# A decode block on one core: TensorE's and VectorE's programs inside a loop of two turns whose first turn jumps over the body, and six filler products for ten

## The chip, the cores and the metric

The kernel runs on one NeuronCore of a Trainium2 chip. The core has five engines that run programs of their own and meet at semaphores: TensorE (PE in the profile, with its weight loads as PEld), VectorE (DVE), ScalarE (ACT), GpSimd (POOL) and SyncE (SP, which here only issues DMAs). [...] 

The metric is the device time of one execution, in microseconds. Before the change the median of 3 runs is 1276.88 us (1276.62 to 1277.0).

## What is computed

One decode step of a transformer block for 4 sequences (B = 4, one new token each, D = 512): layer norm, attention over a cache of 8192 positions with 32 heads of width 128, a residual, a second layer norm, a gated unit of width 1792, and a second residual.

```python
def _A_ref(x, k_cache, v_cache, wq, wo):          # x is normed, (4, 1, 512)
    q = (x @ wq).reshape(B, Sq, 32, 128).transpose(0, 2, 1, 3)
    scores = jnp.einsum("bhqd,bhkd->bhqk", q, k_cache) * (128 ** -0.5)
    o = jnp.einsum("bhqk,bhkd->bhqd", softmax(scores), v_cache)
    return o.transpose(0, 2, 1, 3).reshape(B, Sq, 4096) @ wo
def _B_ref(x, w_gate, w_up, w_down):
    return (sigmoid(x @ w_gate) * (x @ w_up)) @ w_down
h = x + _A_ref(layernorm(x), k_cache, v_cache, wq, wo)
return h + _B_ref(layernorm(h), w_gate, w_up, w_down)
```

All tensors are bfloat16. The two caches hold 4 x 32 x 8192 x 128 elements each; with the weights, each execution has to read 550.77 MB.

## The kernel before, in words

**Data.** The 128 pairs of sequence and head are worked in 32 units of four heads. A unit's K is one DMA, and so is its V. Three slots (`KV`) take them: K alternates between slots 0 and 1, V goes to slot 2, and the last V to slot 0. SP issues everything in one hand-written order: `wq` first (line 532), then K and V units in turn (line 541), each behind a wait until its slot is free, then 40 empty instructions, and at the end `wo` (line 546), `w_gate` (548), `w_up` (552) and `w_down` in three pieces of eight, four and two of its fourteen column tiles (557).

**A unit.** VectorE transposes K in 16 chunks (line 335), TensorE multiplies each with the query (344), VectorE and ScalarE make the softmax (362 to 369), VectorE transposes the weights (375). TensorE multiplies the weights of the unit before with its V (405); ScalarE scales the result (410) and TensorE adds it into one bank (415).

**The programs.** Each engine's instructions are collected in a list (`_Prog.list`), and at the end `play` writes each list into that engine's own program, once. TensorE's and VectorE's programs hold loops over the units: TensorE's body is one unit, 31 turns, with a small loop for the 16 chunks in it; VectorE's is two units, 15 turns. The first unit, the last one (for VectorE) and all that follows the attention stand behind or ahead of these loops as straight code. An engine's program therefore has a start (layer norm, query projection), a loop in which nearly all the time passes, and an end.

**The end.** After the last K unit TensorE runs 24 filler products (`filler(2, 12)`: a product of constants into an unused bank, two in each turn of a small loop, line 388), multiplies the last V (405), lays the attention's output out (415, 454, 461, 466), runs ten filler products (`filler(2, 5)`, called at line 467), multiplies with `wo` (475), adds the residual (479, 480), runs ten more (`filler(2, 5)`, line 481), and goes on with the second layer norm (273 to 287), the gate and up products (492), the sigmoid (503), the product of the two with its transposes in two halves (509, 512) and the product with `w_down` (521), whose fourteen tiles wait for the three pieces of `w_down`. VectorE and ScalarE copy the result (529, 530), ScalarE issues the output DMA (559), and SP waits for it.

Of the kernel before, what the change touches and what calls it, by code (L numbers as in the profile page):

```python
# [18 lines left out]
class _Prog:  # L19
# [52 lines left out]
    def emit(self, eng, fn, waits=(), incs=1, ch=None):  # L72
        todo = self._waits(eng, waits)
        key = ch or eng
        tok = self.token(key, incs) if incs else None
        self._put(eng, todo, key, fn, incs, 1)
        return tok
# [41 lines left out]
def bass_sequential_preLN__mha_block_cached__glu_gated_glu__decode_kernel(  # L119
# [34 lines left out]
    prog = _Prog({"p2d": "dve", "d2d": "dve", "a2d": "dve", "d2p": "pe", "a2p": "pe",  # L154
                  "d2a": "act", "p2a": "act",
                  "k0": "dve", "k1": "dve", "v2": "pe"})
    emit = prog.emit

    with ExitStack() as es:
# [222 lines left out]
        def filler(n, turns=1):  # L382
            if turns > 1:
                prog.open("pe")
            for _ in range(turns):
                if turns > 1:
                    prog.begin("pe")
                emit("pe", lambda e: [e.matmul(bank[XS], Lq[:, 0:128], Lq[:, 0:512], start=True, stop=True) for _ in range(n)][-1],  # L388
                     [t_ps0, t_lq[NU - 1]], incs=0)
                if turns > 1:  # L390
                    prog.end("pe")
            if turns > 1:
                prog.close("pe")
# [70 lines left out]
            return ins  # L464
        t_rt = emit("pe", f, [t_oa])
        t_ot = emit("dve", lambda e: e.tensor_copy(OT, bank[QB[0]][:, 0:B * WOJ]), [t_rt])
        filler(2, 5)

        emit("act", lambda e: e.activation(dummy[:, 0:1], mask[:, 0:1], ACT.Sqrt), [t_mask])

# [89 lines left out]
        emit("sp", lambda e: e.nop(), [t_out], incs=0)  # L560

        for name, e in (("pool", nc.gpsimd), ("act", nc.scalar), ("dve", nc.vector), ("pe", nc.tensor), ("sp", nc.sync)):
            prog.play(nc, name, e)


# [26 lines left out]
```

## Time and profile before

| what | value |
|---|---|
| median of 3 runs | 1276.88 us |
| the profiled execution's own time | 1276.83 us |
| its span, first to last instruction | 1275.6 us |
| mean granted TensorE clock | 0.815 |
| PE, PEld, DVE, ACT, POOL busy | 61%, 26%, 60%, 5%, 0% |
| bytes moved, mean rate | 550.83 MB, 432 GB/s |

The profile is of one execution. Its span starts with the first instruction of the kernel and ends with the last; the execution's own time is 1.23 us longer. Times in the timeline and in the chain of waits are microseconds from the start of the span: first the start, then the duration. In brackets stands how long the engine had been idle and what ended it. A view of windows cuts the span into stretches and gives for each the busy time of the engines, the granted TensorE clock (1.00 is full speed), the mean busy share of the sixteen DMA engines and the rate.

### The profile page before, as it was taken

To read this page: it belongs to the slowest core of one execution; us is meant where nothing else is said; L and a number is where in the kernel's file an instruction comes from. 1 tells how busy PE (TensorE), PEld (TensorE's weight loads), DVE (VectorE), ACT (ScalarE), POOL (GpSimd) and SP (SyncE) were. 2 spreads that over 40 slices of the span, in tenths; PEclk is the share of its full clock that TensorE was granted. 3 is DMA by queue.
4 is the path that set the end of the run, shared out by engine and by line. 5 is a ranking of instruction groups with operands and counts; after the bars stand their busy time and mean duration, and the time that the engine had idled before them with its cause. 6 is when DMAs were issued, how large, how long until landed. Compare 5 with 4: busy or idle time off the path is not lost.

```text
span 1275.6 us, 14073 instructions
## 1 busy us (share of the span) xinstructions
PE 779.7 (61%) x4588; PEld 328.5 (26%) x4636; DVE 762.3 (60%) x917; ACT 59.0 (5%) x114; POOL 5.7 (0%) x22
## 2 busy tenths in 40 slices
PE   1676755557755557655567655567555577555577
PEld 0232222223222223222222222222222232222233
DVE  1876665556665557665567655566655566655571
ACT  2000000000000000000000000000000000000001
POOL 1000000000000000000000000000000000000000
PEclk8888877788877788877788777788777888777888
DMA  9999999999999999999999999999999999999998
GB/s 423 432 426 430 427 450 434 430 430 427 454 430 430 430 427 454 432 427 430 430 452 432 427 430 434 450 430 427 430 440 444 430 427 430 442 442 430 430 427 371
DMA packets 10244, 550.83 MB, mean 432 GB/s; under 512 B 1144, under 2 KB 1152, under 8 KB 1408
## 3 DMA queue, kind: packets, MB, share of 16 engines
q1 hardware_dynamic: 10224, 550.77, 99.7%
q8 instruction: 2, 0.03, 0.0%
q10 hardware_dynamic: 16, 0.01, 0.0%
q14 instruction: 2, 0.02, 0.0%
HBM read 550.77 MB, written 0.00 MB: 432 GB/s over the span
## 4 chain that ended last, share of the span: by engine, by line
DMA 60%; PE 20%; DVE 12%; issue 2%; ACT 1%; SPq 0%; DVEq 0%
DMA KV<-in_A_k_cache_dram 58%; PE PS L344 14%; DVE kT L335 12%; PE PS L405 5%; DMA KV<-in_B_w_down_dram 3%; ACT kT L410 1%; PE PS L415 0%; SPq L541 0%; DVE PTz L375 0%; PE PS L521 0%; DVE KV L529 0%; SPq L557 0%; DVEq L112 0%
## 5 line engine op out<-in xcount | busy, mean ns | idle before, releaser
L344 PE MATMUL PS<-kT,Lq 128*128 128x512 bf16 x2048 | 588.7, 420 | 343.5 <-DVE kT L335 326.4
L335 DVE STREAM_TRANSPOSE kT<-KV 128x1024 f32<-128x1024 f32 x512 | 614.4, 1232 | 300.3 <-DMA KV<-in_A_k_cache_dram 237.5
L344 PEld LDWEIGHTS PS<-kT,Lq 128*128 x2048 | 210.3, 103 | 694.6 <-issue 621.7
L375 DVE STREAM_TRANSPOSE PTz<-E_sb 32x512 bf16<-32x512 bf16 x128 | 89.9, 703 | 129.1 <-PE PS L415 125.5
L405 PE MATMUL PS<-KV,PTz 128*16 128x512 bf16 x2048 | 117.0, 381 | 0.0
L379 PE MATMUL PS<-part,headw 128*128 128x2 f32 x64 | 18.8, 363 | 100.4 <-DVE PTz L375 100.4
L369 ACT ACTIVATE E_sb<-PS,negm 128x512 bf16<-128x512 f32 x32 | 22.0, 687 | 1139.4 <-DVE negm L367 1139.4
L405 PEld LDWEIGHTS PS<-KV,PTz 128*16 128x16 bf16 x2048 | 58.9, 111 | 56.3 <-issue 13.6
L415 PE MATMUL PS<-lane,kT 128*128 128x4 f32 x256 | 33.6, 255 | 31.0 <-ACT kT L410 31.0
L362 DVE TENSOR_REDUCE part<-PS 128x1 f32<-128x512 f32 x32 | 22.1, 691 | 38.7 <-PE PS L344 38.7
L415 PEld LDWEIGHTS PS<-lane,kT 128*128 128x128 f32 x256 | 31.0, 191 | 46.2 <-issue 44.8
L379 PEld LDWEIGHTS PS<-part,headw 128*128 128x128 f32 x64 | 16.0, 310 | 103.7 <-DVE PTz L375 103.7
L410 ACT ACTIVATE kT<-PS,rsb 128x512 f32<-128x512 f32 x32 | 22.0, 687 | 61.5 <-PE PS L405 61.5
L388 PE MATMUL PS<-Lq 128*128 128x512 bf16 x27 | 11.0, 462 | 2.9 <-issue 2.5
L328 DVE TENSOR_TENSOR Lq<-q_all,mask 128x32 bf16<-128x32 bf16 x32 | 9.5, 297 | 0.0
L454 DVE TENSOR_TENSOR kT<-PS,mask 128x512 bf16<-128x512 f32 x1 | 0.7, 692 | 13.3 <-PE PS L415 13.3
L367 DVE STREAM_TRANSPOSE negm<-mxr 128x32 f32<-128x32 f32 x32 | 6.8, 212 | 1.1
L364 DVE STREAM_TRANSPOSE turn<-part 128x32 f32<-128x32 f32 x32 | 6.8, 211 | 1.1
L388 PEld LDWEIGHTS PS<-Lq 128*128 128x128 bf16 x44 | 4.8, 116 | 8.3 <-issue 6.1
L322 PEld LDWEIGHTS PS<-Lq,headw 128*128 128x128 bf16 x32 | 3.5, 108 | 12.8 <-issue 11.3
L396 DVE RECIPROCAL rsb<-PS 128x1 f32<-128x1 f32 x32 | 6.3, 197 | 0.7 <-PE PS L379 0.7
L301 PE MATMUL PS<-KV,kT 128*4 128x512 bf16 x32 | 3.6, 627 | 5.0 <-DMA KV<-in_A_wq_dram 5.0
(70 smaller groups left out, 56.7 us busy)
## 6 DMA issues: line engine op xcount, KB each, us to landing
KV<-in_A_wq_dram SPq DMA_DIRECT2D x1, 4096.0 KB, 12.2
KV<-in_A_wo_dram SPq DMA_DIRECT2D x1, 4096.0 KB, 27.2
KV<-in_B_w_gate_dram SPq DMA_DIRECT2D x1, 1792.0 KB, 31.1
KV<-in_B_w_up_dram SPq DMA_DIRECT2D x1, 1792.0 KB, 34.9
KV<-in_B_w_down_dram SPq DMA_DIRECT2D x1, 1024.0 KB, 32.1
KV<-in_A_k_cache_dram SPq DMA_DIRECT2D x32, 49.6
KV<-in_A_v_cache_dram SPq DMA_DIRECT2D x32, 30.7
KV<-in_B_w_down_dram SPq DMA_DIRECT2D x1, 512.0 KB, 32.9
```

Source lines behind the costliest of these rows:

```text
L328: t_lq[u] = emit("dve", lambda e, ix: e.tensor_tensor(dst, bass.AP(raw(q_all), at(ix, 0) * (4 * TU) + 4 * (u - TU * t), [[NU * 4, 128], [1 ...
L335: t_tr[u, c] = emit("dve", lambda e: e.transpose(kT[:, (c % 2) * TW:(c % 2 + 1) * TW], KVw[:, o:o + TW]), w, ch="d2p")
L344: ins = e.matmul(bank[SBK], bass.AP(raw(Lq), ix[-1] * 2 + (128 * t + c % 2), [[528, 128], [1, 128]]), rhs, start=False, stop=False, skip_g ...
L362: a = emit("dve", lambda e: e.tensor_reduce(part[:, 0:1], bank[SBK], AX.X, ALU.max), [t_sc[u, NT - 1], t_pool], ch="d2d")
L364: a = emit("dve", lambda e: e.transpose(turn_[:, :], part[:, :]), [a], ch="d2d")
L369: t_exp[u] = emit("act", lambda e: e.activation(E_sb[:, :], bank[SBK], ACT.Exp, bias=negm[:, 0:1], scale=SCALE, accum_out=part[:, 1:2]), [ ...
L375: return [e.transpose(PTz[32 * q:32 * (q + 1), :].rearrange("p (r q c) -> p r q c", r=4, q=4)[:, :, q, :], E_sb[32 * q:32 * (q + 1), :].re ...
L379: t_sum[u] = emit("pe", lambda e: e.matmul(bank[QB[1]][:, 0:2], headw[:, :], part[:, 0:2], start=True, stop=True), [t_ptz[u], t_selc], ch= ...
L388: emit("pe", lambda e: [e.matmul(bank[XS], Lq[:, 0:128], Lq[:, 0:512], start=True, stop=True) for _ in range(n)][-1], [t_ps0, t_lq[NU - 1] ...
L405: made.append(e.matmul(PS[32 * j:32 * j + 16, ob:ob + 512], lhsT, KV[:, slot * SLOT + 512 * k:slot * SLOT + 512 * (k + 1)], start=(k < 4), ...
L410: t_ocp[u] = emit("act", lambda e: e.activation(O_sb, bank[OBK], ACT.Copy, scale=rsb[:, 0:1]), [t_pv[u], t_rs[u]], ch="a2p")
L415: ins = e.matmul(bass.AP(raw(PS), at(ix, 0) * 4 + (512 * EX + 4 * (u - t)), [[4096, 128], [1, 4]]), O_sb[:, 128 * q:128 * (q + 1)], lane[: ...
```

## The change

Each of TensorE's and VectorE's programs is put inside a loop of two turns (`Fori(0, 2)`, on that engine alone). In it, a comparison of the turn's number with 1 guards the whole body: in the first turn (number 0) the engine branches over the body to the end of the loop, adds one to the counter and branches back to the top; in the second turn it runs the body once, as before. The other three programs are as they were. No semaphore, wait, buffer or order of instructions inside the bodies changes, but for one line: the filler loop ahead of the product with `wo` has three turns of two products in place of five.

```diff
@@ -464,7 +464,7 @@
         t_ot = emit("dve", lambda e: e.tensor_copy(OT, bank[QB[0]][:, 0:B * WOJ]), [t_rt])
-        filler(2, 5)
+        filler(2, 3)
@@ -560,7 +560,12 @@
         for name, e in (("pool", nc.gpsimd), ("act", nc.scalar), ("dve", nc.vector), ("pe", nc.tensor), ("sp", nc.sync)):
-            prog.play(nc, name, e)
+            if name in ("dve", "pe"):
+                with nc.Fori(0, 2, engines=OrderedEngineSet([e.engine])) as turn:
+                    with e.If_eq(e.to_reg(turn), 1):
+                        prog.play(nc, name, e)
+            else:
+                prog.play(nc, name, e)
```

## The prediction

> **What bounds the kernel now.** I read the page first: its rows of DMA and its queues.
>
> ```profile
> span 1275.6 us, 14073 instructions
> ...
> DMA  9999999999999999999999999999999999999998
> ...
> q1 hardware_dynamic: 10224, 550.77, 99.7%
> q8 instruction: 2, 0.03, 0.0%
> ...
> q14 instruction: 2, 0.02, 0.0%
> ```
>
> The sixteen DMA engines are busy in every slice, and the tensors' queue fills 99.7% of their time. No engine's compute is near that (PE 61%). Two things outside the tensors' queue are to be seen: four instruction packets within the execution, two of 16 KB (0.03 MB over 2) and two of 8 KB (0.02 MB over 2). They are the engines' code, fetched while the program runs, by the same sixteen DMA engines.
>
> Next, the chain that ended last, in order of time, and windows cut through the start and the end.
>
> ```profile
> 1239.80 32.91 DMA KV<-in_B_w_down_dram
> 1272.71 0.04 issue
> 1272.75 0.60 PE PS L521 x8
> 1273.36 0.04 issue
> 1273.39 0.43 PE PS L521 x4
> 1273.82 0.02 issue
> 1273.85 0.41 DVE KV L529
> ```
> ```profile
> 0.00:2.00 2.00, 0.00 (x0) 0.00 (x0) 0.00 (x0) 0.60 (x1) 1.04 (x11) 1.00 0.40 100
> 2.00:4.00 2.00, 0.58 (x1) 0.07 (x1) 0.85 (x2) 1.99 (x4) 1.38 (x6) 1.00 0.91 328
> 4.00:1236.00 1232.00, 751.93 (x4340) 315.53 (x4375) 753.59 (x898) 49.04 (x99) 3.32 (x6) 0.81 1.00 434
> ...
> 1271.00:1271.50 0.50, 0.00 (x0) 0.00 (x0) 0.47 (x3) 0.00 (x0) 0.00 (x0) 1.00 0.93 365
> 1271.50:1272.00 0.50, 0.37 (x8) 0.34 (x10) 0.47 (x2) 0.00 (x0) 0.00 (x0) 1.00 0.32 123
> 1272.00:1272.50 0.50, 0.50 (x14) 0.32 (x8) 0.18 (x1) 0.00 (x0) 0.00 (x0) 1.00 0.14 53
> 1272.50:1273.00 0.50, 0.42 (x10) 0.21 (x8) 0.00 (x0) 0.00 (x0) 0.00 (x0) 1.00 0.12 45
> 1273.00:1275.60 2.60, 0.74 (x12) 0.15 (x6) 0.41 (x1) 0.38 (x1) 0.00 (x0) 1.00 0.01 2
> ```
>
> The last product (L521) waits for the last piece of w_down, and what follows it is fixed: 1275.6 - 1273.39 = 2.21 us. So the end is set by when the last DMA engine finishes. The second figure from the right is the DMA share. From 4 us on it is 1.00. At the end it falls in steps: 0.93 until 1271.5, then 0.32, and from 1272 to 1273 0.14 and 0.12, which is two engines of sixteen (2/16 = 0.125). Fourteen engines are done by about 1271.9; **two are late by about 1.1 us**, and the kernel waits for them. Each engine carries the same number of tensor packets (10224/16 = 639), so those two did something more. I read the trace's list of packets for it (queue, start, duration, bytes):
>
> ```
> q14    63.12  0.31   8192
> q8     87.43  0.92  16384
> q14  1207.71  0.31   8192
> q8   1257.52  0.97  16384
> ```
>
> Two 16 KB fetches, two late engines: that they are the same engines I infer, since in the packet list the engine of each 16 KB fetch starts its next tensor packet about 0.9 us late. q8 should be TensorE's queue: its straight code is by far the longest, and the two fetches fall into the first pass of its loop and into its end, so each page is fetched once and kept.
>
> **The change, part by part.**
>
> *Start: the jump and the jump back.* Each of the two engines runs a counter move, a compare with a branch over the body, an add and a branch back, before its first useful instruction. No row has the price of a jump to code that isn't there. Bounds: 0 where the target is loaded; upward, the shortest DMA round trip shown at an empty queue, x's, issued at 0.80 and used at 2.41, so 1.6 us, for two such trips (there and back) 3.2 us, and twice that, 6.4 us, if each fetches two pages. What covers it:
>
> ```profile
> 0.80 0.57 ACTq L235 DMA_DIRECT2D KV<-in_A_x_dram  x1
> ...
> 2.41 0.68 DVE L273 BATCH_NORM_STATS2 kT<-KV 4x6 f32<-4x512 bf16 x1 [2.41 <-DMA KV<-in_A_x_dram]
> ...
> 13.00 3.59 PE L301 MATMUL PS<-KV,kT 128*4 128x512 bf16 x32 [5.04 <-DMA KV<-in_A_wq_dram]
> ...
> 32.27 2.37 DVE L335 STREAM_TRANSPOSE kT<-KV 128x1024 f32<-128x1024 f32 x2 [14.21 <-DMA KV<-in_A_k_cache_dram]
> ```
>
> TensorE idles 5.0 us for wq, and after the query VectorE idles 14.2 us for the first K. The first loads are issued by SP and ACT, which don't jump. The one DMA that waits on the late engines is the first V's (SP, behind the query's products), which lies in the queue behind two K of 49.6 us to landing. So I cost the start at 0; without that cover it would be 0 to 6.4 us. Later the guarded body runs as before: the three instructions at the end of the loop run under the output DMA.
>
> *The fetches move.* In the first turn TensorE touches the end of its program at about 1 us, where the DMA share is 0.40 (0 to 2 us) and 0.91 (2 to 4 us): 16 x (2 x 0.60 + 2 x 0.09) = 22 us of idle engine time, where a fetch of 0.97 us fits. If the code stays loaded until it runs, both 16 KB fetches leave the busy stretch. Bounds: a gain of 1.1 us (both late engines end with the others: last data at 1271.9 for 1273.0), or none (the fetch starts after 2 us, costs its engine the same, and that engine is late all the same). VectorE's own 8 KB fetch moves with it and is worth nothing: its engine isn't among the last two. I take three quarters, 0.8 us: the fetch is triggered about 1 us before the tensors' first packets, but a second page would be fetched after them.
>
> *Six fillers for ten.*
>
> ```profile
> 1233.33 0.33 SPq L546 DMA_DIRECT2D KV<-in_A_wo_dram  x1
> ...
> 1259.98 0.15 PEld L388 LDWEIGHTS PS<-Lq 128*128 128x128 bf16 x1 [0.28 <-issue]
> ...
> 1260.41 0.15 PEld L388 LDWEIGHTS PS<-Lq 128*128 128x128 bf16 x1 [0.27 <-issue]
> ...
> 1261.82 2.22 PE L475 MATMUL PS<-KV,kT 128*4 128x512 bf16 x32
> ...
> 1268.18 0.21 PEld L283 LDWEIGHTS PS<-ident,kT 4*128 4x128 bf16 x4 [0.56 <-DVE kT L277]
> ...
> 1271.77 0.41 DVE L512 STREAM_TRANSPOSE KV<-KV 128x224 bf16<-128x224 bf16 x1
> ```
> ```profile
> KV<-in_A_wo_dram SPq DMA_DIRECT2D x1, 4096.0 KB, 27.2
> ```
> ```profile
> 1258.20:1261.82 3.62, 2.68 (x7) 0.62 0.95 402
> 1261.82:1262.50 0.68, 0.68 (x9) 0.50 0.98 422
> 1262.50:1264.10 1.60, 1.54 (x28) 1.00 1.01 430
> ```
>
> A filler takes 0.43 us (1260.41 - 1259.98), so four fewer end 1.71 us earlier, at 1260.11 for 1261.82. Then wo is the limit: issued at 1233.33, landed 27.2 us later, at 1260.5. L475 starts at about 1260.6, 1.2 us earlier. The clock (0.50, then 1.00) rises at 1262.5 now, 4.3 us after the products began. If it rises then too, L475 runs 1.9 us of its 3.59 us at the low clock (3.59 is the same 32 products cold, L301), and the remaining 47% at the high one, whose full length is 1.54/0.81 = 1.90 us (0.68/3.59 = 19% had been done by 1262.5): 0.9 us. It ends at 1263.4 for 1264.04, **0.65 us earlier**, and everything to the end of TensorE's chain shifts with it. By itself this is worth 0, since the last w_down piece lands no earlier. It is needed for the first gain: the last transpose (L512) ends at 1272.18, and seven of the fourteen tiles follow it; by the steps of L521 (0.60 us for x8, 0.43 us for the closing x4) these take about 1.1 us, so without the shift the chain would end at 1273.3 and hold the gain to 0.55 us. With it, at 1272.6. A bound below: if the clock rises later, L475 ends at 1260.6 + 3.59 = 1264.2, 0.15 us later than now.
>
> *Sum.* Own time 1276.83: start 0, fetches -0.8, fillers 0 beyond that: 1276.0. The median of the runs shown is 0.05 above the profiled execution; the forecast is **1276.1 us**, with its own range 1275.6 to 1276.5.
>
> **The rivals.**
>
> *A: the fetch is paid anyway* (or doesn't move). For it: the share is 0.91 already from 2 us, TensorE's program has more than one page to fetch, and the jump lands on the last only; the fetch at 87 us may belong to a page in the middle, which the jump doesn't touch, and one late engine is enough. Against: 22 us of idle engine time lie right where the jump is. Time: 1276.88, less at most 0.1: 1276.8.
>
> *B: more fetches than before.* The jump to the end and back drops pages that the body then needs, so that they are fetched twice. Price: one 16 KB fetch makes its engine end 1.1 us late; two on one engine, 2.2 us, so 1276.88 + 1.1 = 1278.0; each further one on the same engine 1.1 more, and from the third on it is slower by over 0.2%. For it: the loop's first pass did have to fetch a page. Against: TensorE's loop branches back 30 times and only two 16 KB packets are listed, so pages that have been left are kept. [...]
>
> *C, the slower one: TensorE stays at the low clock.* Place: between the sixth filler's end (1260.1) and wo's landing (1260.5) TensorE is idle for about 0.4 us, and if that restarts the 4.3 us, the rise comes after L475. Then L475 ends at 1264.2 (+0.15), the ten fillers behind L480 take 10 x 0.43 = 4.3 us for 2.33 and hold up L283 by about 2.0, and gate and up, 1.69 us now, take 3.59/2.22 as long, +1.0. Sum +3.1, less the 0.5 us that the chain has until the last piece: 1279.5. It decides once the gap is long enough to reset the clock; before, gaps of 0.87 and 0.79 us around L415 and L461 stood ahead of the low clock, so 0.4 us is near. Against: L475 is full work itself, and the window before the rise was not gapless either (2.68 us of 3.62 busy).
>
> ```profile
> 1256.14 0.97 PEld L415 LDWEIGHTS PS<-lane,kT 128*128 128x128 f32 x8 [1.36 <-ACT kT L410]
> ...
> 1257.98 0.27 PE L461 MATMUL PS<-laneb,kT 128*128 128x32 bf16 x4 [0.79 <-DVE kT L454]
> ...
> 1265.78 2.33 PE L388 MATMUL PS<-Lq 128*128 128x512 bf16 x10
> ...
> 1268.74 1.69 PE L492 MATMUL PS<-KV,kT 128*4 128x448 bf16 x32 [0.27 <-DVE kT L287]
> ```
>
> **How the numbers follow.** Chances: the forecast 0.46, A 0.34, B 0.14, C 0.04, and 0.02 for a gain larger than I can work out. Within 0.2% (2.55 us, about what a measurement of this kernel tells from no change: 1274.3 to 1279.4) lie the forecast, A and all of B but 0.02: 0.92. Slower: C and that 0.02, 0.06. Faster: 0.02. The range goes from 1275.4 (the full 1.1 us and 0.3 for the scatter of runs) to 1278.2 (B with one further fetch); it leaves out C, the upper part of B and the largest gains, some 0.15.
>
> **What would show it.** Right: q8's packets gone or before 4 us; the DMA share at the end falling to nothing at about 1271.9 with no step of 0.12; L475 at about 1260.6 at clock 0.50, then a rise near 1262.5; L521's last wait ended by VectorE or by w_down at about 1272.3. A: the step of 0.12 still there. B: three or more packets on q8, or a step longer than 1.1 us. C: L492 over 2.5 us. The start is wrong if the first K transpose comes after 32.3 us. The prediction is wrong altogether if the stretch from 4 to 1236 us no longer has a DMA share of 1.00.

## The result and the profile after

| kernel | median | lowest to highest | runs |
|---|---|---|---|
| before | 1276.9 us | 1276.6 to 1277.35 | 22 |
| after | 1278.76 us | 1276.87 to 1279.87 | 22 |

The ratio is 1.0014 (95% interval 1.0007 to 1.002): the change makes the kernel slower by 0.14%, 1.86 us. That is less than the 0.2% that the prediction put as its line, but the interval leaves out 1, and the time lies outside the predicted range (1275.4 to 1278.2). The times also scatter more: over 3.0 us, for 0.75 before. The profiled execution of after took 1277.93 us (span 1276.7), so the views below show 1.1 of the 1.86 us.

The end of the chain of waits of after looks as it did before, only 1.09 us later (the last wait for w_down ends at 1274.48 for 1273.39):

```profile
1240.95 32.86 DMA KV<-in_B_w_down_dram
1273.81 0.04 issue
1273.85 0.60 PE PS L521 x8
1274.46 0.03 issue
1274.48 0.43 PE PS L521 x4
1274.91 0.02 issue
1274.94 0.41 DVE KV L529
```

The instruction packets of after, from the trace's packet list (queue, start, duration, bytes), show that the loop does what it says:

```
q8     4.24  0.92  16384
q14    5.10  0.31   8192
q8     9.87  0.96  16384
q14 1207.46  0.31   8192
```

A page here is what one such fetch brings. TensorE's two pages and VectorE's one are fetched at the start, and none of them a second time; the 8 KB packet at 1207 us is there in every run (1207.71 before), whichever program stands in a loop. Windows through the end (the figure next to the last is the DMA share, the last one GB/s):

```profile
1272.50:1273.00 0.50, 0.31 (x6) 0.30 (x8) 0.33 (x1) 0.00 (x0) 0.00 (x0) 1.00 0.97 389
1273.00:1273.50 0.50, 0.50 (x14) 0.36 (x8) 0.00 (x0) 0.00 (x0) 0.00 (x0) 1.00 1.02 397
1273.50:1274.00 0.50, 0.37 (x10) 0.13 (x6) 0.00 (x0) 0.00 (x0) 0.00 (x0) 1.00 0.28 102
1274.00:1274.20 0.20, 0.20 (x8) 0.14 (x4) 0.00 (x0) 0.00 (x0) 0.00 (x0) 1.00 0.03 10
```

The long step of two late engines is gone: the share goes from 1.02 to 0.28 to 0.03 in a microsecond. Read alone this is the gain that was forecast. But by the packet list the sixteen engines now end 1.9 us later on average (about 1273.7 for 1271.8), and the last one 1.1 us later (1274.1 for 1273.0). The rate from 60 to 100 us points to the place, first before, then after:

```profile
60.00:100.00 40.00, 29.96 (x157) 12.31 (x160) 29.66 (x34) 1.47 (x3) 0.00 (x0) 0.82 1.03 443
```
```profile
60.00:100.00 40.00, 30.87 (x157) 12.43 (x158) 30.53 (x36) 1.47 (x3) 0.00 (x0) 0.83 0.98 421
```

The row says that something is missing there, not how much: one 64 KB packet more or less on each engine (16 x 64 KB in 40 us) is 26 GB/s of such a window. The packet list says how much. Before, sixteen packets are under way at every moment of it. After, engines are without a packet between 89.5 and 91.2 us, 0.84 us each on average, and the first packets behind this gap take longer, which is another 0.5 us each. In between lies the issue of two transfers by SP. Timeline before and after, SP and the first work of TensorE and VectorE on what was loaded (before's two such rows stand in the prediction):

```profile
53.38 0.33 SPq L541 DMA_DIRECT2D KV<-in_A_k_cache_dram  x1
86.88 0.33 SPq L541 DMA_DIRECT2D KV<-in_A_v_cache_dram  x1
87.25 1.47 SPq L541 DMA_DIRECT2D KV<-in_A_k_cache_dram  x1
```
```profile
14.72 3.58 PE L301 MATMUL PS<-KV,kT 128*4 128x512 bf16 x32 [6.46 <-DMA KV<-in_A_wq_dram]
34.00 2.37 DVE L335 STREAM_TRANSPOSE kT<-KV 128x1024 f32<-128x1024 f32 x2 [14.21 <-DMA KV<-in_A_k_cache_dram]
55.49 0.33 SPq L541 DMA_DIRECT2D KV<-in_A_k_cache_dram  x1
89.42 0.33 SPq L541 DMA_DIRECT2D KV<-in_A_v_cache_dram  x1
89.79 0.43 SPq L541 DMA_DIRECT2D KV<-in_A_k_cache_dram  x1
```

The products with wq start 1.7 us later (14.72 for 13.00), the first K lands 1.7 us later (34.00 for 32.27), the third K is issued 2.1 us later (55.49 for 53.38) and the second V 2.5 us later (89.42 for 86.88). SP issues in order, so the fourth K stands behind that V, and between the third K and this moment no transfer is added to the queue. Before, the second V came just in time; after, the packet list has most engines without a packet for 0.3 to 1.7 us, until 90.4 to 91.2 us. I call this a dry queue.

The packet list also shows why wq is late: thirteen of its sixteen parts are done at 12.2 to 12.8 us, as before (12.2 to 12.6), the other three at 13.2, 13.7 and 14.2, and three fetches lie in that stretch. Of the 2.5 us by which the second V is late, the first K explains 1.7. The other 0.8 arise on the way: in each of the first two units VectorE waits for TensorE once more than before (0.46 and 0.45 us). What makes it wait there was not tried; the late start below has the same waits without a fetch.

### The profile page after: what moved, and what is told of

It is laid out like the page before. It is cut to its first block, busy times and chain, and to the rows that moved or that the text cites. A ratio compares the mean times of both kernels' runs of the same rounds, so it can differ in the third digit from the quotient of the medians.

```text
span 1276.7 us, 14127 instructions
## 1 busy us (share of the span) xinstructions
PE 800.6 (63%) x4632; PEld 327.9 (26%) x4632; DVE 762.0 (60%) x917; ACT 58.9 (5%) x114; POOL 5.7 (0%) x22
## 5 line engine op out<-in xcount | busy, mean ns | idle before, releaser
L322 PE MATMUL PS<-Lq,headw 128*128 128x512 bf16 x32 | 18.8, 586 | 10.8 <-issue 9.5
## 6 DMA issues: line engine op xcount, KB each, us to landing
KV<-in_A_k_cache_dram SPq DMA_DIRECT2D x32, 49.6
```

Source lines behind the costliest of these rows:

```text
L322: emit("pe", lambda e: e.matmul(bank[bk], headb, zeros, start=True, stop=False, skip_group_check=True), waits, incs=0)
```

## The experiments

**Theory 1.** The fetches at 4 to 10 us each hold up one DMA engine (0.92, 0.31 and 0.96 us). The first product with wq waits for wq's last part (14.2 us, the product at 14.72, thirteen parts by 12.8), so wq and the first K land late; the work from the first K to the second V's issue has nothing to spare; the queue runs dry near 90 us, and this kernel, whose DMA share before is 1.00 from 4 to 1236 us, doesn't get that back. **Rivals:** the fillers; the late start of TensorE and VectorE in itself (TensorE's first product began at 7.46 for 2.43 us); some other effect of code in another place.

All times are medians of eleven runs (eight for the last experiment); the ratio is to the kernel before measured beside them (1276.92 to 1276.98 us), with its 95% interval.

**Six fillers alone.**

```diff
-        filler(2, 5)
+        filler(2, 3)
```

> Six fillers for ten, no loop of two turns. Theory 1 (the fetches that the first turn triggers at 4 to 10 us make wq and the first K land late, the work up to the issue of the second V and fourth K (86.88 us before, 89.42 after) is late by as much, and the DMA queue runs dry near 90 us): nothing of this happens here, 1276.9 us, the last w_down piece sets the end as before, and the two late DMA engines are still there. Rival (the fillers: TensorE colder or the product with wo later): 1278.8 us with this edit alone.

1276.92 us, ratio 1.0001 (0.9992 to 1.001), and the second V issued at 86.96 us. The fillers are not the cause of the 1.86 us. But four of its eleven runs lie at 1277.6 to 1277.7, above all 33 of before beside them (1277.42 at most). None of the four was profiled, and why they are longer is open. In the timeline of the profiled run (1276.90 us) the product with wo starts when wo has landed, as forecast, and still takes 3.16 us:

```profile
1260.68 3.16 PE L475 MATMUL PS<-KV,kT 128*4 128x512 bf16 x32 [0.35 <-DMA KV<-in_A_wo_dram]
```

**The loops with ten fillers.**

```diff
-            prog.play(nc, name, e)
+            if name in ("dve", "pe"):
+                with nc.Fori(0, 2, engines=OrderedEngineSet([e.engine])) as turn:
+                    with e.If_eq(e.to_reg(turn), 1):
+                        prog.play(nc, name, e)
+            else:
+                prog.play(nc, name, e)
```

> The loops of two turns, with ten fillers as before. Theory 1: as slow as the whole change, 1278 to 1279.5 us, with a dry stretch near 90 us. Rival (fillers): 1276.9 us. The end should have the DMA engines finishing together; TensorE's later L475 may then cost up to 0.6 us more.

1277.98 us (1276.53 to 1278.69), ratio 1.0006 (0.9997 to 1.0015): just under the expected band in the median, with an interval that still takes in 1; nine of its eleven runs are over 1277.5 us, of before's 33 none. The profiled run, 1278.69, issued its second V at 88.49 us and has a dry stretch of 0.67 us per engine. Its DMA engines don't finish together, as was expected: the DMA share is 0.71, 0.62, 0.40 and 0.08 in the half microseconds from 1273 to 1275 us.

**A late start without a fetch.** TensorE and VectorE run a small loop of empty instructions first.

```diff
+            if name in ("dve", "pe"):
+                with nc.Fori(0, 24, engines=OrderedEngineSet([e.engine])):
+                    e.nop()
             prog.play(nc, name, e)
```

> No loop of two turns; TensorE and VectorE each run a small loop of 24 empty instructions first, so that they start some us late without any fetch. Theory 1: wq and the first K land as before (13.0 and 32.27 us), 1276.9 us. Rival (the late start of the two engines itself, L290 at 7.43 for 2.43 us): 1278 us or more, with the second V issued about 2.5 us later.

1276.96 us, ratio 1.0 (0.9991 to 1.0009), though TensorE began later than in the change:

```profile
9.81 0.58 PE L290 MATMUL PS<-KV,ident 4*4 4x512 bf16 x1 [9.81 <-issue]
...
12.99 1.03 PE L301 MATMUL PS<-KV,kT 128*4 128x512 bf16 x8 [2.38 <-DMA KV<-in_A_wq_dram]
```

It still waits for wq, and the first K lands as before (32.26 us). As a cause by itself that rival is out. But the late start was not without effect: the second V went out at 87.79 us, 0.9 us later than before, with one more wait for TensorE in each of the first two units. That used up most of the slack and cost no time.

**One engine's loop at a time**, `("pe",)` and `("dve",)` in the edit above, ten fillers.

> Only TensorE's program in a loop of two turns, ten fillers. Theory 1, TensorE's 16 KB fetches being what delays wq and K: 1278 to 1279.5 us, as with both. If VectorE's 8 KB fetch or its late start mattered: clearly less than with both.

> Only VectorE's program in a loop of two turns, ten fillers. Its fetch of 8 KB moves from 63 us to the start. Theory 1: a delay of wq and K of 0.8 us or less, under the 1 to 2 us by which the second V was in time: 1276.9 us (to 1277.3), with TensorE's fetches at 87 and 1257 us and the two late engines as before.

TensorE's alone: 1278.22 us, ratio 1.0009 (1.0 to 1.0018), second V at 89.45 us in its profile. VectorE's alone: 1276.88 us (1276.72 to 1279.65), ratio 1.0004 (0.9995 to 1.0013). The median is that of before, but four of its eleven runs are over 1277.5, and the profiled one, 1278.33, issued its second V at 88.13 us. Of before's 33 runs beside it, two came to 1278.25 and 1278.62, so part of this tail may not be the edit's. One 8 KB fetch brings the kernel to the edge, TensorE's two of 16 KB carry it over.

**The fetch's load without the jump.** Two rows of 16 KB are read from `wo` into an unused place at the start; each is a single packet on one engine, where wq is cut over all sixteen (before's list has sixteen of its packets starting between 1.81 and 2.74 us, while x and the result come in four packets of 1 KB each). A line that isn't shown lets SP wait for both rows ahead of the first V; they have landed by 11.2 us, and that V goes out at 17.7 us, behind the query's products as before.

```diff
+        for i in range(2):
+            prog.dma("act", "xr", lambda e, i=i: e.dma_start(reg(2, 16384, 8192)[i:i + 1, :],
+                     A_wo.rearrange("(p j) f -> p (j f)", p=128)[i:i + 1, 0:8192]), tok=t_xr)
```

> No loop; two extra rows of 16 KB are read right after x into a place that isn't used yet, two packets on one or two DMA engines beside wq. It does what the fetches do to the DMA engines, without touching a program. Theory 1: wq and the first K land 0.6 to 1.4 us late, the second V is issued later by as much or more, a dry stretch near 90 us where the delay is over about 1.5 us: 1277.5 to 1279 us. Rival (the jump itself, or code that is loaded in another place): 1276.9 to 1277.5 us, the time of the extra bytes at most.

1278.21 us (1276.77 to 1279.28), ratio 1.0009 (1.0 to 1.0018). No program was put in a loop, and the kernel slows down as with TensorE's loop: seven of the eleven runs took over 1278 us, of before's 33 two. The profiled run does not have the loss (1276.94 us): its first K was late by 1.0 us (33.26) and its second V issued at 87.77 us, and there was no dry stretch.

**Only the second V's issue late.** SP runs a loop of 8 or of 3 empty turns behind the wait for the slot.

```diff
+            if n == 4:
+                emit("sp", lambda e: e.nop(), [w], incs=0)
+                prog.open("sp")
+                for _ in range(8):
+                    prog.begin("sp")
+                    emit("sp", lambda e: e.nop(), incs=0)
+                    prog.end("sp")
+                prog.close("sp")
```

> No loop of two turns, start as before; SP runs a small loop of 8 empty turns between the wait for the second V's slot and its DMA, so that this DMA and the fourth K's behind it are issued some 2 to 3 us later, and nothing else changes. Theory 1: what the change does comes through this one issue, so 1278 to 1279.5 us, with a dry stretch near 90 us. Rival (the damage is done to the DMA engines at the start, and the dry stretch is only its sign): 1276.9 us.

> The same with 3 empty turns, 0.8 to 1.1 us. Theory 1 with a point from which it decides (about 88.0 us for the issue): at or just under it, so between 1276.9 and 1277.8 us, some runs dry and some not.

With 8 turns: 1278.72 us, ratio 1.0014 (1.0005 to 1.0023), the whole loss of the change from one late issue, with a start like before's (first K at 32.20 us). The issue moved by 1.5 us, less than the 2 to 3 expected:

```profile
88.42 0.33 SPq L549 DMA_DIRECT2D KV<-in_A_v_cache_dram  x1
```

With 3 turns: 1277.46 us (1276.89 to 1278.15), ratio 1.0004 (0.9995 to 1.0013), in between as expected. The profiled run took 1277.01 us. The profiled runs so far, in the order of this issue, with the time that a DMA engine is without a packet from 60 to 100 us (from the packet list, mean of the sixteen):

| profiled run | second V issued, us | engine without a packet, us | time of the run, us |
|---|---|---|---|
| before | 86.88 | 0 | 1276.83 |
| six fillers | 86.96 | 0 | 1276.90 |
| two reads of 16 KB | 87.77 | 0 | 1276.94 |
| late start | 87.79 | 0 | 1277.24 |
| 3 empty turns | 87.90 | 0 | 1277.01 |
| VectorE's loop | 88.13 | 0.22 | 1278.33 |
| 8 empty turns | 88.42 | 0.59 | 1278.21 |
| loops, ten fillers | 88.49 | 0.67 | 1278.69 |
| after | 89.42 | 0.84 | 1277.93 |
| TensorE's loop | 89.45 | 0.89 | 1279.61 |

The point lies near 88 us: before's 86.88 had about 1.1 us to spare.

**The early chain given room.** The first K comes in two DMAs, and VectorE starts on the half that it reads first.

```diff
+            if n == 0:
+                prog.dma("sp", "k0a", lambda e, src=src: e.dma_start(reg(0, SLOT // 2, SLOT // 2), src[:, SLOT // 2:]), tok=t_k0a)
+                prog.dma("sp", "k0", lambda e, src=src: e.dma_start(reg(0, 0, SLOT // 2), src[:, :SLOT // 2]), tok=toks[x, u])
+                continue
...
-            w = [toks["k", u], ...
+            w = [t_k0a if u == 0 and c < NT // 2 else toks["k", u], ...
```

> No loop; the first K comes in two DMAs of half its size, and VectorE starts on the first half when it has landed (near 22 us for 32 us). The early chain then runs some us ahead. Theory 1: no change by itself, 1276.9 us, since the queue wasn't dry before; the second V is issued well ahead of 86.88 us or the queue's next need. The fetches at 87 and 1257 us and the two late engines stay.

> The whole change, with the first K in two halves. Theory 1: the early chain has several us to spare, the queue doesn't run dry near 90 us, and the loss goes: 1276.9 us, or 1276.0 if the moved fetches then leave the end without two late engines. Rival (anything else in the loop costs the time): 1278.8 us as with the change.

Alone: 1276.75 us, ratio 0.9998 (0.9989 to 1.0007). With the whole change: 1276.82 us, ratio 0.9998 (0.9989 to 1.0007). The loss is gone, and so is most of the scatter (1276.53 to 1277.75; as with the six fillers alone, two runs lie at 1277.6 and 1277.75). SP's row and the end, in windows, of the change with the split:

```profile
80.25 0.33 SPq L546 DMA_DIRECT2D KV<-in_A_v_cache_dram  x1
```
```profile
1271.50:1272.00 0.50, 0.48 (x10) 0.42 (x12) 0.42 (x2) 0.00 (x0) 0.00 (x0) 1.00 0.35 135
1272.00:1272.50 0.50, 0.50 (x12) 0.22 (x6) 0.00 (x0) 0.00 (x0) 0.00 (x0) 1.00 0.18 70
1272.50:1273.00 0.50, 0.35 (x8) 0.25 (x8) 0.00 (x0) 0.00 (x0) 0.00 (x0) 1.00 0.11 41
```

The second V goes out 9.2 us earlier than in after, the queue isn't dry, and the two late engines at the end (0.11) are back, although their fetches were at 4.05 and 10.12 us. So the even end of after was no gain from the move. Its dry stretch had done it: in the packet list of after the engines reach the end of the queue between 89.5 and 91.5 us, and the first packets behind it all end between 93.5 and 94.1. The engines that were behind caught up in that pause. A shorter one did not bring this: with the ten-filler loops (0.67 us) and the 8 empty turns (0.59 us) the engines finish one after the other over some 2 us (1273.0 to 1274.9, and 1272.5 to 1274.4).

**Fetches into idle DMA engines.** The same, with SP held for 12 empty turns ahead of wq.

```diff
+        prog.open("sp")
+        for _ in range(12):
+            prog.begin("sp")
+            emit("sp", lambda e: e.nop(), incs=0)
+            prog.end("sp")
+        prog.close("sp")
         prog.dma("sp", "wq", ...
```

> The whole change with the first K in halves, and SP runs 12 empty turns (3 to 4 us) ahead of its first DMA, so that TensorE's fetches meet idle DMA engines. If a fetch in idle time costs its engine nothing: all 16 engines end within about 0.6 us of each other, and the time is 1276.8 + 3 to 4 - 1.1, so about 1279 us. If the late engines at the end have another cause: two are late by 1.1 us all the same, and it is about 1280.3 us.

1280.19 us, ratio 1.0025 (1.0015 to 1.0036), wq issued 3.0 us later (3.81 for 0.81). TensorE's first page came at 2.09 us, ahead of the tensors, its second at 9.53 us among them. The end, in windows:

```profile
1274.00:1274.50 0.50, 0.00 (x0) 0.03 (x1) 0.47 (x2) 0.00 (x0) 0.00 (x0) 0.78 0.77 295
1274.50:1275.00 0.50, 0.49 (x6) 0.34 (x8) 0.14 (x1) 0.00 (x0) 0.00 (x0) 0.50 0.19 74
1275.00:1275.50 0.50, 0.50 (x8) 0.28 (x6) 0.00 (x0) 0.00 (x0) 0.00 (x0) 0.50 0.06 25
1275.50:1276.00 0.50, 0.50 (x10) 0.30 (x6) 0.00 (x0) 0.00 (x0) 0.00 (x0) 0.50 0.06 25
```

0.06 is one engine of sixteen: of the two late engines one is left, and one is enough to set the end (1276.0 us, the others by 1275.0). Neither expectation was met whole; each holds for one fetch. The fetch into idle time left no late engine, the one among the tensors one that is 1.1 us late and more. The packets don't name their engine; this goes by their number. The time is over the first expectation also because the low clock (0.50) met the last product in the profiled run (1280.72 us), and it ran 3.15 us for 2.15.

No version is faster than before by what the runs can tell; the split alone and with the change are level with it.

## Why the prediction was wrong

**The bound and the two late engines: right.** DMA bounds the kernel to the last packet, and there are as many late engines as 16 KB fetches among the tensors: two before (share 0.12) and two in the change with the split (0.11). Held SP shows it from the other side: with one fetch out of the busy stretch, one late engine is left (0.06).

**The jump and what covers it: right as far as it went.** TensorE began at 7.46 for 2.43 us, within the bound of 6.4 us on the cost (its two pages for each trip were an assumption that no run shows), and starting late costs no time by itself (late start, 1276.96 us). Its first q8 packet ended at 5.16 us (4.24 + 0.92), 2.3 us ahead of that product; what the 5.0 us consist of was not shown. Both pages fetched at the start still served at the end, 1.25 ms later: after's list has no third q8 packet.

**"So I cost the start at 0": the step that failed.** The prediction asked when TensorE and VectorE would be late, and counted their waits for wq (5.0 us) and the first K (14.2 us) as cover. It took the landing of wq and K as fixed. But the fetch sits on the engines that bring them (three of wq's sixteen parts end at 13.2 to 14.2 us, the others by 12.8), and a wait for a DMA covers nothing that makes the DMA itself late. For the second V it looked at the wrong issue: the first V has two K of 49.6 us ahead of it, as it said, but the second V, at the end of the chain from the first K's landing, goes out with about 1.1 us to spare. That slack could be worked out from the trace of before, and wasn't. Up to the third K, wq and four units are queued, 4.2 + 4 x 8.4 = 37.7 MB by their shapes; at 434 GB/s that is 87 us from the first packets at 1.8 us, so by this estimate the queue is dry at about 89 us. The first packets follow an issue by 1.0 us (wq, 0.81 to 1.82), so the second V had to be issued by about 88 us, and it was at 86.88. The prediction's own sign for a wrong start, the first K transpose after 32.3 us, came: 34.00. Its sign for the gain, no step of 0.12 at the end, came too, but some 2 us later than forecast and for another reason, the dry stretch.

**The fetches move, "I take three quarters": 0 in place of 0.8.** The packets came at 4.24 and 9.87 us, in the busy stretch, not at about 1 us into idle time; the row of x (1.6 us from issue to use) was read at an empty queue, while the code's packet came only when the tensors filled the engines (4.24 us, their first packets at 1.81); with SP held the first came at 2.09. By the split version, with the queue never dry, the move is worth 1276.82 against 1276.75 us, nothing. Rival A was right on this step, and its price too.

**Six fillers: the mechanism right, the size off.** L475 started when wo had landed, at 1260.68 in the run with this edit alone. But L475 took 3.16 us there and ended at 1263.84, 0.2 us earlier for the 0.65 forecast, inside the bound below: by the prediction's lengths (3.59 us at the low clock, 1.90 us at the high one) the clock rose at about 1263.4, an estimate, and not at 1262.5. It was worth 0 by itself in the median, as forecast. Rival C's low clock behind L475 is in no profiled run; a low clock near the end came in the held run alone, at the last product.

**Rival B** had the sign and nearly the time (1278.0) for another reason: no page is fetched twice, so the nearness is luck. The slower side needed a mechanism that none of the rivals had, a queue that runs dry.

## What to carry to other kernels

In a kernel that DMA bounds, the slack to work out is not when an engine gets its data but when each transfer is issued against when the queue has run out; here one issue had 1.1 us to spare, and the late landing of the first K went through to it. Before moving any load to the start, name the transfers that share its DMA engines and what is chained to their landing. And an even finish of the DMA engines can be a sign of a pause earlier in the run rather than of better balance: compare the time at which they finish, too.

## What was not expected of the hardware

- In the profile of after the pause cost more than its length. An engine is without a packet for 0.84 us on average; the first 64 KB packets behind the pause take up to 3.26 us for 2.42, another 0.5 us per engine; and many up to about 220 us take 2.45 to 2.6 us, 0.4 us more in sum. What lengthens them was not tried.
- In the profiled run of TensorE's loop alone one DMA engine restarted at 92.7 us, when the other fifteen were back by 90.9, and ended at 1275.8, some 2 us behind the others. Why that engine stayed behind is open; it is the slowest of that kernel's eleven runs (1279.61 us).
- A fetch of 16 KB held its DMA engine for longer than a tensor read of the same bytes: 0.92 to 0.97 us among the tensors (1.36 us at 2.09 us with SP held), where each 16 KB read of `wo` took 0.61 us, and the next tensor packet started about 0.9 us late.
